# Merging B's value and output weights in seven PSUM banks instead of ten

## The chip, the core and the metric

The kernel runs on one core of a Trainium2 chip. The core has TensorE (PE in the profile; its weight loads are the row PEld), VectorE (DVE), ScalarE (ACT), GpSimd (POOL) and SyncE (SP, which here only issues DMAs). The metric is the time of one execution on the device in microseconds. Three runs of the kernel before took 254.32, 254.86 and 255.46 us; their median, 254.86 us, is the time before.

## What is computed

Two attention blocks, A and B, each on its own input of 2048 tokens and 640 features, with 32 heads of 20 features; their outputs stand side by side in the result. A is causal attention in a window of 256 keys. B is linear attention, which needs no softmax over keys:

```python
phi = lambda t: jnp.where(t > 0, t + 1, jnp.exp(t)) + 1e-6
pq, pk = phi(q), phi(k)
kv = jnp.einsum("bhsd,bhse->bhde", pk, v)
z = jnp.einsum("bhsd->bhd", pk)
num = jnp.einsum("bhqd,bhde->bhqe", pq, kv)
den = jnp.einsum("bhqd,bhd->bhq", pq, z)[..., None] + 1e-6
o = num / den
return (lambda x, *d: x.transpose(*d))(o, 0, 2, 1, 3).reshape(B, S, D) @ wo
```

## The kernel before

For B, the small matrix kv of each head (20 by 20) is known before any query is needed. So the kernel multiplies kv into the output weights once, head by head, and gets one merged weight matrix of 640 by 640. The output of B is then (phi(q) divided by its denominator) times that matrix. The function b_merge makes the merged matrix. Its 640 rows are cut into five chunks c of 128. Heads are kept in groups of six (120 rows), so a chunk overlaps two groups, and each product is two matmuls that add up in one PSUM bank: the transposed kv (kv_T) is the stationary operand, the output weights (wo) stream past it. A bank holds 512 fp32 columns. The kernel before makes the 640 columns of a chunk in two halves of 320, one bank each: ten banks, twenty matmuls, ten copies out of PSUM into w_sb["B"] (the tile wB).

All dense work of the kernel passes through the same four PSUM banks (the pool dps, tiles called dense): query, key and value projections, B's sums, the merge, the output projections, and the value products of A. Each user takes a bank with bank(), fills it on PE, and an ACT or DVE instruction copies it out and so frees it. When no bank is free, PE stands. The copy goes through evac, which keeps a running load for ACT and for DVE, in columns, and picks ACT while its load is less than DVE's plus AHEAD (600); each copy adds its columns plus COPY (160). A bank of B's query or key projection is freed later than others: phi first has ACT take the exponential (e, L286), and then DVE makes two passes (L290 on e, L293 from the bank), so it is free only after the second pass.

The order of the work is written by the kernel itself. A's scores are made in 76 tiles (S_ps, L791), which have the other four banks: PE fills them, ACT takes one exponential over all four (p, L799, the longest ACT instruction), and only then may PE write the next tile's scores. POOL masks p (L814). Two tiles later PE multiplies p with the values (L838). In the gaps between tiles PE gets dense work from a plan: the calls at(t0, t1, gen, n) spread the n banks of a generator evenly over plan times t0 to t1, one unit being about a tile; all entries are sorted by time. A credit in matmul columns is given per tile, and take() draws banks from the sorted list until it is used up, also cutting a chain of matmuls in the middle, so that a bank may begin before a score tile and end behind it. Every chain yields the columns it cost; End marks the end of a bank. The query chain of B that belongs to plan times 45 to 50 (b_q(1)), the merge, A's value projection and A's output projection alternate around the merge.

SP issues all DMAs in one queue, in the order in which the program posts them; soon() holds a DMA back until some more banks were begun. Among them are the transposes of B's phi(q) into rows by token (tok<-phi, L708), those of the finished quotients (xA<-tok, L760), those of A's normalised values (oT<-N, L879), and the reload of B's input from scratch (xB<-x_scr, L955, 640 KB). DVE multiplies tok with the reciprocal denominators (L756), and needs all five transposes of a block of 512 tokens for that.

The program as built fixes on each engine the order of all instructions, and for each chain which of the four banks it gets and so which copy it waits for.

Of the kernel before, what the change touches and what calls it, by code (L numbers as in the profile page):

```python
# [9 lines left out]
P = 128  # L10
# [7 lines left out]
DH = 20  # L18
HV = DH + 1
NG = H // 4  # L20
SB = 512
# [71 lines left out]
def kernel(  # L93
# [10 lines left out]
    nc = tc.nc  # L104
    _, S, D = A_x.shape
    KT = D // P
# [34 lines left out]
    w_sb = {}  # L141
    wo_sb = {}
# [63 lines left out]
    GH = 6  # L206
# [20 lines left out]
    def flush(before=None):  # L227

        while later and (before is None or later[0][0] <= before):
            later.pop(0)[1]()  # L230
# [9 lines left out]
    def settle(all=True):  # L240
        while posts and (all or posts[0][0] <= begun[0]):
            posts.pop(0)[1]()
# [12 lines left out]
    def evac(dst, src, n=SB, to=None):  # L255

        if to is None:
            to = "A" if load["A"] < load["D"] + AHEAD else "D"
        load[to] += n + COPY
        if to == "A":  # L260
            nc.scalar.activation(out=dst, in_=src, func=ACT.Copy)  # L261
        else:
            nc.vector.tensor_copy(out=dst, in_=src)

    def bank(wide=False):
        flush(begun[0] - 2)
        begun[0] += 1
        settle(False)
        if wide:
            return dps.tile([P, 2 * SB], BF16, name="dense")  # L270
        return dps.tile([P, SB], F32, name="dense")
# [49 lines left out]
    for c in range(KT):  # L321
        m = EXTRA * c
        while m < EXTRA * (c + 1):
            n = min(EXTRA * (c + 1) - m, DH - m % DH)
# [198 lines left out]
    GD = GH * DH  # L523
    NGR = KT + 1
    PAD = GD
    G = w_sb["B"][:, :, D : 2 * D]
    kv_T = wp.tile([P, NGR, PAD + GD + 8 * KT], BF16, name="kv_T")
# [139 lines left out]

    def b_merge():

        for c in range(KT):  # L670
            for lo in (0, D // 2):
                cols = slice(lo, lo + D // 2)
                ps = bank()
                for i in range(2):

                    at = PAD + (P - GD) * c - i * GD
                    nc.tensor.matmul(  # L677
                        ps[:, 0 : D // 2],
                        lhsT=kv_T[0:GD, c + i, at : at + P],
                        rhs=wo_sb["B"][0 : GH * DH, c + i, cols],  # L680
                        start=(i == 0),
                        stop=(i == 1),
                    )
                evac(w_sb["B"][:, c, D + lo : D + lo + D // 2], ps[:, 0 : D // 2], D // 2)
                yield End(D)

    oT_B = {}

# [57 lines left out]
    def quotients(s):  # L746


        def one(tb):
            settle()  # L750
            add_load(d=1400)
            if tb == 0:
                oT_B[s] = xp.tile([P, KT, SB], BF16, name="xA")
            v = tok_of[s][:, tb, 0:D]
            vh = v.rearrange("p (h e) -> p h e", e=DH)
            nc.vector.tensor_tensor(  # L756
                out=vh, in0=vh, in1=rden_of[s][:, tb, :, :].to_broadcast([P, H, DH]), op=ALU.mult
            )
            out = oT_B[s][:, :, tb * P : (tb + 1) * P]
            soon(lambda: nc.sync.dma_start_transpose(out=out, in_=v), 1)  # L760

        quotients_due.extend((s, tb, one) for tb in range(TPS))
# [274 lines left out]
    def at(t0, t1, gen, n):  # L1037
        for i in range(n):
            plan.append((t0 + (i + 0.5) / n * (t1 - t0), gen, i == n - 1))

    def do(t0, t1, fns):
        fns = list(fns)
        for i, fn in enumerate(fns):
            plan.append((t0 + (i + 0.5) / len(fns) * (t1 - t0), None, fn))
# [30 lines left out]
    for s, tq, td, tx in ((0, (39.5, 45), 46.3, 47.7), (1, (45, 50), 53, 54.3),  # L1075
                          (2, (52, 57), 59.4, 60.4), (3, (58, 61.6), 63.9, 64.4)):
        at(*tq, b_q(s), KT)
        at(td, td + 0.1, b_den(s), 1)
        do(tx, tx, [lambda s=s: quotients(s)])
    at(46.0, 52.8, b_merge(), 2 * KT)  # L1080
    for n, s, t0, t1 in (("A", 0, 44.5, 48.5), ("A", 1, 50.2, 54.8), ("B", 0, 54.8, 59.2),
                         ("B", 1, 60.2, 64), ("A", 2, 64.4, 68.2), ("B", 2, 69, 73),
                         ("B", 3, 73, 76)):
# [40 lines left out]
    for i, (s, parts, selects, done) in enumerate(units):  # L1124
        p = scores(s, parts, selects)
# [6 lines left out]
        if ready and ready[0][0] + LAG <= i:  # L1132
# [3 lines left out]
            _, at = ready.popleft()  # L1136
# [10 lines left out]
    while ready:  # L1147
        take(5500)
        _, at = ready.popleft()
# [36 lines left out]
```

## Time and profile before

| | |
|---|---|
| median of three runs | 254.86 us (254.32 to 255.46) |
| profiled execution | 254.11 us, of which its span is 252.4 us |
| PE busy | 241.7 us (96%), 3681 matmuls |
| ACT, DVE, POOL busy | 196.6, 167.2, 186.3 us (78%, 66%, 74%) |
| granted TensorE clock | full speed in all 40 slices |
| merge on PE (L677) | 20 matmuls, first at 162.4 us, last at 184.4 us |
| merge copies | 6 on ACT (452 ns each), 4 on DVE (474 ns each) |

A row of instructions gives line, engine, operation, names written and read, shapes, count, then busy time and the mean duration in ns of one, and the engine's idle time before it with what ended it. A row of the timeline gives start and length in us first. PE's matmuls are pipelined: a duration holds the way through the array too, so that matmuls that follow each other start closer together than they last, and a short wait can hide in the modelled end of the matmul before. Times between starts are therefore what a matmul costs PE. In the same way an ACT instruction starts somewhat before the one ahead of it ends.

Score tiles are numbered from 1 in this document: tile 51 starts at 161.20 us, tile 52 at 164.15, 53 at 166.97, 54 at 169.97, 55 at 172.78, 56 at 175.85, 57 at 178.75, 58 at 182.15, 59 at 185.05.

### The profile page before, as it was taken

How to read it: one execution, taken by the hardware profiler on the slowest of the kernel's cores; microseconds unless marked ns; L12 is line 12 of the kernel's file. 1: busy time of each engine (PE TensorE's matmuls, PEld its weight loads, DVE VectorE, ACT ScalarE, POOL GpSimd, SP SyncE). 2: the span in 40 equal slices, each digit the busy share in tenths (PEclk: the TensorE clock that was granted, in tenths of full speed). 3: DMA queues.
4: the chain of work that ended last, by engine and by line, in shares of the span. 5: the costliest groups of instructions: out<-in, count | busy, mean ns of one | idle time of the engine just before them, and what ended most of it. 6: DMA issues, size and time to landing. Idle time of an engine off the chain costs nothing.

```text
span 252.4 us, 8729 instructions
## 1 busy us (share of the span) xinstructions
PE 241.7 (96%) x3681; PEld 141.3 (56%) x3727; DVE 167.2 (66%) x311; ACT 196.6 (78%) x194; POOL 186.3 (74%) x310
## 2 busy tenths in 40 slices
PE   7999999999999999998999999999999999999994
PEld 6644456557755555466445555556455565655573
DVE  1345678777654565685664867566979688859662
ACT  3476779889867798996658877889998998999541
POOL 1226897879867898786778969888887978999800
PEclk9999999999999999999999999999999999999999
DMA  6995597799650342995459494731959389588614
GB/s 224 325 252 152 115 207 131 177 279 132 93 100 3 98 138 50 262 249 148 69 110 175 104 192 89 179 46 35 194 110 162 89 186 174 117 163 139 195 56 155
DMA packets 68412, 37.04 MB, mean 147 GB/s; under 512 B 51605, under 2 KB 67349, under 8 KB 68373
## 3 DMA queue, kind: packets, MB, share of 16 engines
q1 hardware_dynamic: 67685, 35.67, 67.2%
q10 hardware_dynamic: 688, 0.82, 0.9%
q8 instruction: 29, 0.48, 0.8%
q14 instruction: 10, 0.08, 0.1%
HBM read 14.42 MB, written 9.83 MB: 96 GB/s over the span
## 4 chain that ended last, share of the span: by engine, by line
PE 87%; issue 4%; ACT 3%; DVE 2%; DMA 2%; SPq 0%; ACTq 0%
PE dense L276 49%; PE S_ps L791 11%; PE dense L838 9%; PE dense L566 8%; PE dense L411 7%; DMA wA<-in_A_wqkv_dram 2%; ACT p L799 1%; PE first L411 1%; DVE phi L293 1%; PE dense L720 1%; DVE e L290 1%; ACT e L286 1%; PE dense L677 1%; PE dense L649 1%; PE dense L905 0%
## 5 line engine op out<-in xcount | busy, mean ns | idle before, releaser
L814 POOL TENSOR_SCALAR_AFFINE_SELECT p<-p 128x256 bf16<-128x256 bf16 (+2 forms) x280 | 176.5, 660 | 42.8 <-ACT p L799 41.3
L799 ACT ACTIVATE p<-S_ps 128x2048 bf16<-128x2048 f32 x76 | 142.8, 1879 | 34.6 <-PE S_ps L791 32.3
L276 PE MATMUL dense<-xA,wqk 128*128 128x512 bf16 x188 | 48.9, 380 | 1.4 <-issue 0.8
L791 PEld LDWEIGHTS <-kpad 20*128 20x128 bf16 (+1 forms) x1216 | 21.7, 98 | 29.6 <-issue 26.0
L791 PE MATMUL S_ps<-qpad,kpad 20*65 20x64 bf16 (+3 forms) x1216 | 33.7, 227 | 0.1
L851 DVE STREAM_TRANSPOSE T<-dense 128x512 f32<-128x512 f32 x32 | 22.8, 712 | 15.7 <-PE dense L838 15.5
L290 DVE TENSOR_SCALAR e<-e 128x512 bf16<-128x512 bf16 x40 | 18.6, 466 | 21.3 <-ACT e L286 21.1
L276 PEld LDWEIGHTS <-wqk 128*128 128x128 bf16 x200 | 17.8, 98 | 19.5 <-POOL wqk L355 0.4
L293 DVE SCALAR_TENSOR_TENSOR phi<-dense,e 128x512 bf16<-128x512 f32 x40 | 27.7, 691 | 1.6
L838 PE MATMUL dense<-p,vA 128*32 128x64 bf16 (+2 forms) x1216 | 25.9, 231 | 0.2
L276 PE MATMUL dense<-wB,xB 128*128 128x128 bf16 (+1 forms) x155 | 25.3, 297 | 0.5 <-issue 0.3
L566 PE MATMUL dense<-tok,phi 128*128 128x129 bf16 (+1 forms) x152 | 24.2, 296 | 1.5 <-issue 1.4
L276 PE MATMUL dense<-xB,wB 128*128 128x512 bf16 x91 | 24.8, 380 | 0.7 <-issue 0.5
L276 PE MATMUL dense<-wo,oT 128*128 128x128 bf16 (+4 forms) x160 | 24.3, 293 | 0.6 <-issue 0.5
L286 ACT ACTIVATE e<-dense 128x512 bf16<-128x512 f32 x40 | 23.6, 598 | 1.2 <-PE dense L276 1.0
L411 PE MATMUL dense<-wA,xA 128*128 128x320 bf16 x140 | 23.8, 300 | 0.3 <-issue 0.2
L276 PE MATMUL dense<-wB,xA 128*128 128x128 bf16 (+1 forms) x153 | 23.0, 296 | 0.6 <-issue 0.5
L838 PEld LDWEIGHTS <-vA 128*32 128x32 bf16 x1216 | 19.4, 97 | 3.8 <-issue 0.8
L261 ACT ACTIVATE osb<-dense 128x512 bf16<-128x512 f32 (+2 forms) x28 | 15.9, 581 | 5.3 <-PE dense L276 5.2
L411 PEld LDWEIGHTS <-xA 128*128 128x128 bf16 x160 | 14.9, 98 | 8.0 <-ACT xA L349 0.4
L868 DVE TENSOR_TENSOR N<-T,recA 128x320 bf16<-128x320 f32 (+1 forms) x28 | 15.5, 553 | 3.4 <-DMA wo<-in_A_wo_dram 2.5
L756 DVE TENSOR_TENSOR tok<-tok,rden 128x640 bf16<-128x640 bf16 x16 | 17.3, 1084 | 0.2 <-DMA tok<-phi 0.2
(66 smaller groups left out, 195.5 us busy)
## 6 DMA issues: line engine op xcount, KB each, us to landing
out_dram<-osb SPq DMA_DIRECT2D x7, 640.0 KB
x_scr<-xB SPq DMA_DIRECT2D x4, 640.0 KB
tok<-in_B_x_dram SPq DMA_DIRECT2D x4, 640.0 KB
xB<-x_scr SPq DMA_DIRECT2D x4, 640.0 KB
wB<-in_B_wqkv_dram SPq DMA_DIRECT2D x3, 800.0 KB
q_scr<-qpad SPq DMA_DIRECT2D x16, 60.0 KB
k_scr<-kpad SPq DMA_DIRECT2D x16, 60.0 KB
qpad<-q_scr SPq DMA_DIRECT2D x16, 60.0 KB
```

What stands on the lines that cost most here:

```text
L276: nc.tensor.matmul(dst, lhsT=lhs(kt), rhs=rhs(kt), start=(kt == 0), stop=(kt == KT - 1))
L286: nc.scalar.activation(out=view(e), in_=src, func=ACT.Exp)
L290: nc.vector.tensor_scalar(out=e[:], in0=e[:], scalar1=1e-6, scalar2=1.0 + 1e-6, op0=ALU.add, op1=ALU.min)
L293: nc.vector.scalar_tensor_tensor(out=dst, in0=src, scalar=0.0, in1=view(e), op0=ALU.max, op1=ALU.add)
L411: nc.tensor.matmul(ps[:, 0 : hh * DH], lhsT=xt[:, kt, tb * P : (tb + 1) * P], rhs=w_sb["A"][:, kt, i * hh * DH : (i + 1) * hh * DH], start ...
L566: nc.tensor.matmul(out, lhsT=pk[:, tb, c * P : (c + 1) * P], rhs=x[:, tb, lo:hi], start=(i == 0), stop=(i == len(blocks) - 1),)
L756: nc.vector.tensor_tensor(out=vh, in0=vh, in1=rden_of[s][:, tb, :, :].to_broadcast([P, H, DH]), op=ALU.mult)
L791: nc.tensor.matmul(S_ps[0:keys, j, col : col + n], lhsT=k_pad[kb // TPS][rows, g, ko : ko + keys], rhs=q_pad[s][rows, g, q0 : q0 + n], sta ...
L799: nc.scalar.activation(out=p, in_=S_ps[:], func=ACT.Exp, scale=scale)
L814: nc.gpsimd.affine_select(out=dst, in_=v, pattern=[[0, 4], [0, n], [sgn, w]], compare_op=ALU.is_ge, fill=0.0, base=base, channel_multiplie ...
L838: nc.tensor.matmul(O_ps[32 * j : 32 * (j + 1), q0 : q0 + n], lhsT=v_flat[kb // TPS % 3][:, at + j * HV : at + j * HV + 32], rhs=p[:, j, co ...
L851: nc.vector.transpose(out=T.rearrange("p b e -> p (b e)"), in_=O_ps[:])
```

## The change

The columns of a chunk are no longer halved. The first 512 columns of each chunk get a bank of their own (five banks). The last 128 columns of chunks 0 to 2 share a sixth bank, those of chunks 3 and 4 a seventh, and each of these two banks is copied out by one instruction over several chunks. A bank of the merge yields End with the columns of its two matmuls per chunk: 1024, 768 and 512 where it was 640. The seven banks are planned over 45.8 to 52.8, so one plan unit apart, where the ten were planned over 46.0 to 52.8.

```diff
+        def product(out, c, cols):
+            for i in range(2):
+                at = PAD + (P - GD) * c - i * GD
+                nc.tensor.matmul(
+                    out,
+                    lhsT=kv_T[0:GD, c + i, at : at + P],
+                    rhs=wo_sb["B"][0 : GH * DH, c + i, cols],
+                    start=(i == 0),
+                    stop=(i == 1),
+                )
         for c in range(KT):
-            for lo in (0, D // 2):
-                cols = slice(lo, lo + D // 2)
-                ps = bank()
-                for i in range(2):
...
-                evac(w_sb["B"][:, c, D + lo : D + lo + D // 2], ps[:, 0 : D // 2], D // 2)
-                yield End(D)
+            ps = bank()
+            product(ps[:], c, slice(0, SB))
+            evac(w_sb["B"][:, c, D : D + SB], ps[:])
+            yield End(2 * SB)
+        for cs in (range(0, 3), range(3, KT)):
+            ps = bank()
+            for i, c in enumerate(cs):
+                product(ps[:, i * P : (i + 1) * P], c, slice(SB, D))
+            evac(
+                w_sb["B"][:, cs[0] : cs[-1] + 1, D + SB : 2 * D],
+                ps[:, 0 : len(cs) * P].rearrange("p (c n) -> p c n", n=P),
+                len(cs) * P,
+            )
+            yield End(2 * len(cs) * P)
...
-    at(46.0, 52.8, b_merge(), 2 * KT)
+    at(45.8, 52.8, b_merge(), KT + 2)
```

More of the change, by code (lines that the diff above doesn't have):

```diff
@@ L668, in b_merge @@
     def b_merge():
-        for c in range(KT):
-            for lo in (0, D // 2):
-                cols = slice(lo, lo + D // 2)
-                ps = bank()
-                for i in range(2):
[L676 to L683, printed above, removed]
-                evac(w_sb["B"][:, c, D + lo : D + lo + D // 2], ps[:, 0 : D // 2], D // 2)
-                yield End(D)
+        def product(out, c, cols):
[8 more added lines that the diff above has]
+                )
+        for c in range(KT):
+            ps = bank()
[12 more added lines that the diff above has]
+            yield End(2 * len(cs) * P)
     oT_B = {}
```

## The prediction

> **What bounds the kernel now.** I read the page's busy times and slices first, then the chain of work that ended last, then the rows by form for the lines that change, and at the end the timeline of 160 to 200 us engine by engine.
>
> ```profile
> PE 241.7 (96%) x3681; PEld 141.3 (56%) x3727; DVE 167.2 (66%) x311; ACT 196.6 (78%) x194; POOL 186.3 (74%) x310
> PEclk9999999999999999999999999999999999999999
> PE 87%; issue 4%; ACT 3%; DVE 2%; DMA 2%; SPq 0%; ACTq 0%
> ```
>
> PE is the bound: busy 96%, the chain runs through it for 87%, at full clock in every slice. So the change is worth the columns it takes off PE, plus the stalls of PE that it removes or makes. Nothing else counts.
>
> ```profile
> L677 PE MATMUL dense<-wo,kv_T 120*128 120x320 bf16 x20 | 4.1, 300 | 0.3 <-DVE phi L293 0.3
> L261 ACT ACTIVATE osb<-dense 128x512 bf16<-128x512 f32 x24 | 14.2, 607 | 1.8 <-PE dense L276 1.7
> L261 ACT ACTIVATE wB<-dense 128x320 bf16<-128x320 f32 x6 | 2.4, 452 | 0.0
> L263 DVE CAST osb<-dense 128x512 bf16<-128x512 f32 x11 | 7.5, 683 | 3.6 <-PE dense L276 3.5
> L263 DVE CAST wB<-dense 128x320 bf16<-128x320 f32 x4 | 1.9, 474 | 0.5 <-PE dense L677 0.5
> ```
>
> The merge has one visible wait, 0.3 us for a bank that phi frees. The timeline shows it, and who is ahead of it on ACT and DVE:
>
> ```profile
> 178.86 0.61 ACT L286 ACTIVATE e<-dense 128x512 bf16<-128x512 f32 x1
> 179.35 1.89 ACT L799 ACTIVATE p<-S_ps 128x2048 bf16<-128x2048 f32 x1
> 180.50 0.69 DVE L293 SCALAR_TENSOR_TENSOR phi<-dense,e 128x512 bf16<-128x512 f32 x1
> 181.11 0.79 ACT L261 ACTIVATE wB<-dense 128x320 bf16<-128x320 f32 x2
> 181.25 0.43 PE L677 MATMUL dense<-wo,kv_T 120*128 120x320 bf16 x2 [0.34 <-DVE phi L293]
> ```
>
> PE stops until phi ends at 181.19. The exponential e of that bank ran before the long exponential p of tile 57.
>
> **The change, part by part.** *Matmuls.* Both kernels issue 20, and 6400 columns: 20 of 320, or 10 of 512 and 10 of 128. What one costs is the distance between starts. These rows (start, length, count) give it:
>
> ```profile
> 222.95 2.76 PE L276 MATMUL dense<-wo,oT 128*128 128x512 bf16 x12
> 171.73 0.84 PE L411 MATMUL dense<-wA,xA 128*128 128x320 bf16 x5
> 204.07 1.28 PE L276 MATMUL dense<-wB,xA 128*128 128x128 bf16 x20
> ```
>
> Less the length of the last one (0.38, 0.30, 0.22): 2.38/11 = 216 ns, 0.54/4 = 135 ns, 1.06/19 = 56 ns. Before: 20 x 135 = 2.70 us; after: 10 x 216 + 10 x 56 = 2.72 us. So 0.0, with bounds of -0.1 and +0.1 (5 ns on each of 20). The Trainium skill (TensorE: Matmul & The Clock Gate, Back-to-back issue gap) speaks against short matmuls: in a stream of load and matmul it gives about 81 ns at 128 columns and 131 ns at 512. By 81 ns the ten short ones would cost 0.25 us more. The rows above disagree at both sizes (56 and 216 ns, each with its own weight load), so that is left out of the sum.
>
> *Copies.* Ten of 320 (6 x 0.452 + 4 x 0.474 = 4.6 us) become three of 512 and one of 384 on ACT (3 x 0.607, and some 0.50, estimated between the two rows) and two of 512 and one of 256 on DVE (2 x 0.683, and some 0.41, on the line through 320 and 512): 4.1 us. The 0.5 us saved lies on engines that are not the bound: 0.0, as long as no bank is late. Each long copy does hold its bank 0.15 to 0.21 us longer.
>
> *The order.* The two built programs' instruction lists differ on PE only from tile 51 to tile 59; POOL's is equal. Three places matter.
>
> (a) Tile 53. At 167.46 the value product waits for ACT's wB copy (166.97 + 0.45 = 167.42): its matmuls follow tile 53's last one by 0.22 us where 0.12 is usual. In the new order that bank is freed earlier by DVE's copy of vA. Gain 0.10 (0 to 0.1).
>
> (b) Tile 57. Up to tile 56 the new order has 16 value matmuls and 6 merge ones of 512 where there were 18 and 8 of 320: 3.47 against 3.54 us. With (a), tile 57 starts at about 178.6. Then comes the difference that I rate highest: the query chain of b_q(1) is cut by tile 57, three matmuls ahead of it and two behind, where all five were ahead. Its e therefore stands behind p on ACT's queue. The new list has there p, e, wB of 512, osb, wB of 384, p. Behind tile 57 PE has the two query matmuls, a merge bank of 512, five of the output projection and the bank with six of 128: 0.36 + 0.43 + 0.43 + 1.08 + 0.34, so that it comes at 181.2 to a chain whose bank is freed by that wB copy. ACT: p starts 0.57 after its score tile (164.15 to 164.72 at tile 52): 179.2; e 1.76 after p (179.35 to 181.11): 180.95; wB 0.49 after e (178.86 to 179.35): 181.45; it ends 0.61 later: 182.05. PE resumes at 182.1 and has lost 0.85 to 0.9. Before, it lost 0.50 here (arrived at 180.75, went on at 181.25) and 0.10 on the next chain, which waited for the first of the two wB copies (181.25 to 181.62, where two matmuls take 0.27). Net +0.25. Bounds: -0.60, if ACT gets to that copy before PE asks, and +0.9, if p of tile 57 slips by one more 512-column copy ahead of it (0.61). I take +0.25: it follows from the listed order.
>
> (c) Later. The different loads make evac deal a few later copies otherwise: one of osb goes to ACT between tiles 65 and 66. There ACT had no gap: a copy at 205.39, then p at 206.10. One more copy (0.49 between starts) makes p of tile 66 0.1 to 0.2 later; it ended at 207.98 and tile 67 started at 208.16. Cost 0.05 (0 to 0.2).
>
> *SP.* One transpose tok<-phi (183.68) moves behind three oT<-N, one xA<-tok and the 640 KB reload xB<-x_scr:
>
> ```profile
> 183.68 1.21 SPq L708 DMA_TRANSPOSE tok<-phi  x1
> 184.94 3.92 SPq L879 DMA_TRANSPOSE oT<-N  x3
> 188.98 2.14 SPq L760 DMA_TRANSPOSE xA<-tok  x1
> 191.22 0.53 SPq L955 DMA_DIRECT2D xB<-x_scr  x1
> 192.19 1.21 SPq L760 DMA_TRANSPOSE xA<-tok  x1
> 192.80 0.78 DVE L756 TENSOR_TENSOR tok<-tok,rden 128x640 bf16<-128x640 bf16 x1
> ```
>
> The first product of that block (L756, 192.80) needs it. Without it in front the queue reaches xB 1.2 us earlier, at 190.0, and the transpose goes at 190.5. By the trace's landing events it landed at 186.1, 2.4 us after its issue; the transpose behind the reload landed at 196.5, 5.3 us after the reload's issue. So it now lands at 192.9 to 195.3, and DVE waits up to 2.5 us. Behind it on DVE stand recA, N, a second L756 (2.4 us from the first start to the end of all), then e and phi of the next query bank (0.39 + 0.69): phi ends at 195.3 + 3.5 = 198.8. PE asks for that bank at 198.79, plus the 0.2 of above. So the cover, DVE's idle 1.37 us before 196.62, is just enough: 0.0, and every us later than 195.4 costs PE 1 us. Bounds 0 and +1.5.
>
> *Sum*: 0.0 - 0.1 + 0.25 + 0.05 + 0.0 = +0.2 us on the profiled execution's 254.11 (span 252.4 and 1.7 around it). That execution is 0.75 us under the median of the runs shown; on the median the sum is 255.05, say 255.1. A difference of 0.5% (1.27 us) is about what a measurement can tell from none; this is a sixth of it.
>
> **The rivals.** *Fewer banks pay (faster).* If the stall of (b) vanishes, because ACT reaches e before p, 0.7 us go (0.60 and 0.10): 254.2. For it: three banks fewer ask for the four. Against it: e's place in ACT's list. It decides where the query chain ends before tile 57's p starts at 179.2. Even this is not 0.5%: PE's stalls for banks in this stretch sum to no more.
>
> *The transpose lands late (slower).* Between 165 and 190 transposes behind a 640 KB transfer took up to 5.1 us from issue to landing (177.81 to 182.94, behind out_dram). Issued at 190.5 to 192, that is 195.6 to 197.1, so PE loses 0.2 to 1.7 us: about 256.4 at the upper end. It decides from a landing after 195.4, and passes 0.5% from 196.5. Against it: nothing was added to the queues, only the order changed.
>
> *Long copies make bubbles (slower).* Five banks are held 0.15 to 0.21 us longer each; if PE stood for every one of them, 5 x 0.2 = 1.0 us, and with the sum 256.1. Against it: PE stood for a merge copy at two places only, tile 53 and behind tile 57, so it is unlikely. The Trainium skill (Perfetto Trace Analysis, Optimizing Scalar/DVE Operations) advises to break up ACT or DVE instructions that are not saturated but make bubbles on other engines, which is the opposite of this change; the wait at 181.62 for a wB copy agrees, with 0.10 us.
>
> **How the numbers follow.** Forecast, no change that can be told (254.4 to 255.7): 0.62. Faster rival 0.13, of which 0.05 over 0.5%. Late transpose 0.17, of which 0.13 over 0.5%. Long copies 0.08, nearly all over 0.5%, counted 0.07. That gives faster 0.05, same 0.75, slower 0.20. The range takes in the gain of 0.7 and 1.4 us of loss around 255.0: 254.2 to 256.4.
>
> **What the profile after would show.** 20 merge matmuls of 216 and 56 ns between starts; no wait before tile 53's value product; PE idle at about 181 to 182, ended by ACT's wB copy; e behind p at tile 57; L756 at 193 to 195.4 released by the DMA tok<-phi, and DVE's idle time before 196.6 gone; PE not idle near 199. A stall of PE there, or a landing after 196, makes the prediction wrong upward; no stall at 182 makes it wrong downward.

## The result and the profile after

The changed kernel takes 255.33 us (median of 22 executions, 254.58 to 257.49). The kernel before, measured beside it, takes 254.47 us (22 executions, 253.06 to 256.18). The ratio is 1.0037, with a 95% interval of 1.0021 to 1.0054: about 0.9 us slower. That is within the 0.5% that were set as the bound of no change, but the interval leaves out 1, so the loss is clear of the noise, and its upper end passes the bound. A second measurement on another chip gave 1.0048 (1.0036 to 1.0060), or 1.2 us.

The page of the changed kernel: busy times, the granted clock in the 40 slices, and the chain of work that ended last by engine.

```profile
PE 249.0 (97%) x3727; PEld 142.1 (56%) x3727; DVE 166.7 (65%) x310; ACT 196.7 (77%) x192; POOL 186.3 (73%) x310
PEclk9999999999999999999999999999999999999999
PE 89%; DMA 5%; DVE 3%; ACT 1%; issue 0%; SPq 0%; DVEq 0%
```

PE is still the bound, at full clock by that row. The page's busy time of PE can't be compared with the one before: 46 matmul records were missing there (3681 of 3727). The chain has DMA 5% and DVE 3%, where both had 2%: of the DMA part 3% is a weight load in the opening (wA) and 2% is tok<-phi, which the chain of before didn't hold.

The groups by form, for the merge and its copies (count, then busy time and mean ns of one):

```profile
L674 PE MATMUL dense<-wo,kv_T 120*128 120x512 bf16 x10 | 3.0, 380 | 0.0
L674 PE MATMUL dense<-wo,kv_T 120*128 120x128 bf16 x10 | 0.9, 218 | 0.0
L261 ACT ACTIVATE wB<-dense 128x512 bf16<-128x512 f32 x3 | 1.8, 599 | 0.0
L261 ACT ACTIVATE wB<-dense 128x384 bf16<-128x384 f32 x1 | 0.5, 522 | 0.0
L263 DVE CAST wB<-dense 128x512 bf16<-128x512 f32 x2 | 1.3, 664 | 0.0
L263 DVE CAST wB<-dense 128x256 bf16<-128x256 f32 x1 | 0.4, 414 | 0.0
```

No merge matmul waits any more. Where the time went is read from the starts of the score tiles, which run from the first to the last stage in both kernels. The profiled execution of the changed kernel is itself the slowest of the 22 (257.49 us): its first score tile starts 2.93 us later than before. One part of that weight load landed 2.0 us later (8.26 us against 6.29), and PE ran at half rate until 10.3 us (a matmul of 320 columns took 267 ns between starts, 136 after that), where before it did so until 4.2; the row PEclk holds no record of that stretch. That has nothing to do with the change: the instruction lists are equal there, and in a second profile of the changed kernel the same tile starts 0.8 us later than before. So every run below is set to zero at the start of tile 51, where the instruction lists begin to differ. Against the kernel before, the changed kernel then stands at -0.16 us at tile 57, +0.22 at tile 58, +0.12 from tile 59 to 63, +1.21 at tile 64 and +1.19 to the end. Two places make the loss, and the timeline shows both (columns: start, length, engine, line, instruction, and in brackets the idle time before it and what ended it):

```profile
181.33 1.88 ACT L811 ACTIVATE p<-S_ps 128x2048 bf16<-128x2048 f32 x1 [0.18 <-PE S_ps L803]
183.11 0.59 ACT L286 ACTIVATE e<-dense 128x512 bf16<-128x512 f32 x1
183.58 0.60 ACT L261 ACTIVATE wB<-dense 128x512 bf16<-128x512 f32 x1
184.24 0.38 PE L276 MATMUL dense<-wo,oT 128*128 128x512 bf16 x1 [0.66 <-ACT wB L261]
...
189.74 1.22 SPq L772 DMA_TRANSPOSE xA<-tok  x1
191.09 1.68 SPq L967 DMA_DIRECT2D xB<-x_scr  x1
192.87 1.21 SPq L720 DMA_TRANSPOSE tok<-phi  x1
194.51 1.20 SPq L772 DMA_TRANSPOSE xA<-tok  x1
198.44 0.82 DVE L768 TENSOR_TENSOR tok<-tok,rden 128x640 bf16<-128x640 bf16 x1 [3.26 <-DMA tok<-phi]
201.44 0.69 DVE L293 SCALAR_TENSOR_TENSOR phi<-dense,e 128x512 bf16<-128x512 f32 x1
202.18 0.81 PE L276 MATMUL dense<-xB,wB 128*128 128x512 bf16 x3 [0.93 <-DVE phi L293]
```

The first group is the wait that the prediction expected at tile 57: e stands behind p, the merge copy behind e, and PE behind the copy. The second is the transpose behind the reload. It is issued at 192.87, lands at 198.2 by the trace's landing events, and DVE has waited 3.26 us for it when it starts the first product of block 1 (L768, the L756 of before). Two products, e and phi later PE gets its bank, 0.93 us late. The kernel before has no wait at these matmuls:

```profile
198.79 0.81 PE L276 MATMUL dense<-xB,wB 128*128 128x512 bf16 x3
```

The queue order changed because a transpose of block 1 is held back by soon() for a number of banks, counted as they are begun. With seven banks in place of ten the same count is reached later in the plan, while the reload is posted at a fixed plan time (51.2) and so passes ahead.

### The profile page after: what moved, and what is told of

Read it like the earlier page. It is cut to its first block, busy times and chain, and to the rows that moved or that the text cites. A ratio compares the mean times of both kernels' runs of the same rounds, so it can differ in the third digit from the quotient of the medians.

```text
span 255.7 us, 8772 instructions
## 1 busy us (share of the span) xinstructions
PE 249.0 (97%) x3727; PEld 142.1 (56%) x3727; DVE 166.7 (65%) x310; ACT 196.7 (77%) x192; POOL 186.3 (73%) x310
## 4 chain that ended last, share of the span: by engine, by line
PE 89%; DMA 5%; DVE 3%; ACT 1%; issue 0%; SPq 0%; DVEq 0%
PE dense L276 50%; PE S_ps L803 10%; PE dense L566 9%; PE dense L850 8%; PE dense L411 7%; DMA wA<-in_A_wqkv_dram 3%; DMA tok<-phi 2%; DVE tok L768 1%; PE first L411 1%; PE dense L732 1%; PE dense L674 1%; PE dense L649 1%; DVE phi L293 1%; ACT e L286 0%; PE dense L917 0%
## 5 line engine op out<-in xcount | busy, mean ns | idle before, releaser
L276 PE MATMUL dense<-xA,wqk 128*128 128x512 bf16 x200 | 50.9, 380 | 0.1
L276 PE MATMUL dense<-xB,wB 128*128 128x512 bf16 x100 | 26.3, 380 | 0.9 <-DVE phi L293 0.9
L276 PE MATMUL dense<-wo,oT 128*128 128x512 bf16 (+4 forms) x165 | 25.3, 296 | 0.7 <-ACT wB L261 0.7
L276 PE MATMUL dense<-wB,xB 128*128 128x512 bf16 (+1 forms) x160 | 25.9, 300 | 0.0
L566 PE MATMUL dense<-tok,phi 128*128 128x129 bf16 (+1 forms) x160 | 25.5, 300 | 0.0
L411 PE MATMUL dense<-wA,xA 128*128 128x320 bf16 x140 | 25.0, 309 | 0.2 <-DMA wA<-in_A_wqkv_dram 0.2
L276 PE MATMUL dense<-wB,xA 128*128 128x512 bf16 (+1 forms) x160 | 24.3, 299 | 0.0
L261 ACT ACTIVATE osb<-dense 128x512 bf16<-128x512 f32 (+2 forms) x30 | 17.0, 580 | 5.4 <-PE dense L276 4.5
L411 PEld LDWEIGHTS <-xA 128*128 128x128 bf16 x160 | 15.5, 101 | 9.0 <-ACT xA L349 0.5
L768 DVE TENSOR_TENSOR tok<-tok,rden 128x640 bf16<-128x640 bf16 x16 | 16.3, 1021 | 3.4 <-DMA tok<-phi 3.3
```

What stands on the lines that cost most here:

```text
L276: nc.tensor.matmul(dst, lhsT=lhs(kt), rhs=rhs(kt), start=(kt == 0), stop=(kt == KT - 1))
L411: nc.tensor.matmul(ps[:, 0 : hh * DH], lhsT=xt[:, kt, tb * P : (tb + 1) * P], rhs=w_sb["A"][:, kt, i * hh * DH : (i + 1) * hh * DH], start ...
L566: nc.tensor.matmul(out, lhsT=pk[:, tb, c * P : (c + 1) * P], rhs=x[:, tb, lo:hi], start=(i == 0), stop=(i == len(blocks) - 1),)
L768: nc.vector.tensor_tensor(out=vh, in0=vh, in1=rden_of[s][:, tb, :, :].to_broadcast([P, H, DH]), op=ALU.mult)
```

## The experiments

Two theories stood against each other. Theory 1: the transpose that lands late makes 1.1 us of the loss (and, as a second part, ScalarE's order at tile 57 makes 0.3 to 0.4 us). Theory 2: the longer banks and copies make it.

**Seven banks, the reload one place later.**

```diff
-    for s, t0, t1 in (..., (3, 30.2, 51.2)):
+    for s, t0, t1 in (..., (3, 30.2, 51.6)):
```

> The seven banks as they are; only the 640 KB reload xB<-x_scr is planned at 51.6 instead of 51.2, which lets the transpose tok<-phi pass ahead of it on SP and moves no other instruction on any engine. Theory 1 (the late transpose is the loss): the transpose is issued near 191.1 instead of 192.87 and lands by 195.2 instead of 198.1, VectorE's wait of 3.26 us ahead of the first value product of block 1 falls under 0.5 us, PE's gap of 0.93 us at tile 64 goes, and the time falls by 0.9 to 1.1 us, to 0.9995 to 1.001 of the kernel before. Theory 2 (the longer banks and copies are the loss): PE's gaps stay where they are, the time stays at 1.0037 of the kernel before. Against both: the reload itself, one place later, becomes late for block 3's first bank; then PE waits for DMA xB there.

Measured: 254.17 us, ratio 1.0004 (0.9990 to 1.0017). The timeline of this kernel, SP and DVE:

```profile
188.77 1.91 SPq L720 DMA_TRANSPOSE tok<-phi  x1
190.78 0.53 SPq L967 DMA_DIRECT2D xB<-x_scr  x1
...
192.80 0.78 DVE L768 TENSOR_TENSOR tok<-tok,rden 128x640 bf16<-128x640 bf16 x1
```

The transpose lands at 191.9 and DVE starts the product at 192.80 without a wait, as in the kernel before. By tile starts the kernel goes through tile 64 unchanged at +0.12 and ends at +0.10. On the changed kernel's clock, which is 2.3 us later here, the transpose is issued at 191.1 and lands at 194.2, as expected. The reload lands at 195.4 in its own profile and is late for nobody. So the swap of two neighbours on SP is worth the whole 1.09 us, and being behind three oT<-N and one xA<-tok costs nothing.

**Ten banks, the transpose behind the reload.** The mirror: the kernel before, with only this DMA held back.

```diff
...
-            phi(pq[:, c, :], ps[:], then=lambda fn=to_tokens: soon(fn, 2))
+            phi(pq[:, c, :], ps[:], then=lambda fn=to_tokens, late=(s, c) == (1, KT - 1):
+                held_back.append(fn) if late else soon(fn, 2))
...
         nc.sync.dma_start(out=xB[NS + s].rearrange("p k n -> p (k n)"), in_=x_scr[s])
+        s == 3 and held_back.pop()()
```

> The kernel before, its ten banks untouched; only the fifth transpose tok<-phi of block 1 is held back until the reload xB<-x_scr has been issued, so that SP's order is the changed kernel's and every other engine's order is the one of before. Theory 1: the transpose lands near 196 instead of 186.1, VectorE waits for it 2.5 to 3.5 us, PE loses 0.9 to 1.2 us near tile 64, and the time is 1.0035 to 1.005 of the kernel before. Theory 2: no change, 0.999 to 1.001.

Measured: 255.01 us, ratio 1.0046 (1.0027 to 1.0065). The timeline of this kernel:

```profile
189.04 1.42 SPq L955 DMA_DIRECT2D xB<-x_scr  x1
190.51 1.20 SPq L708 DMA_TRANSPOSE tok<-phi  x1
...
195.82 0.83 DVE L756 TENSOR_TENSOR tok<-tok,rden 128x640 bf16<-128x640 bf16 x1 [2.94 <-DMA tok<-phi]
...
199.56 0.81 PE L276 MATMUL dense<-xB,wB 128*128 128x512 bf16 x3 [0.61 <-DVE phi L293]
```

Without any of the new banks the same wait comes, at the same place. By tile starts the loss is 0.77 us, all of it between tiles 63 and 64; the product starts at 195.82. The size is a little under what was expected by the profile, within it by the times. With both directions shown, theory 2 is out for this part.

**More bytes ahead of the late transpose.**

```diff
...
         nc.sync.dma_start(out=xB[NS + s].rearrange("p k n -> p (k n)"), in_=x_scr[s])
+        s == 3 and nc.sync.dma_start(out=more, in_=x_scr[s][:, 0 : KT * SB // 2])
```

> The changed kernel with one more copy of 320 KB, from DRAM to a DRAM buffer that nothing reads, issued on SP between the reload and the late transpose. It computes nothing else. Theory 1: the issue adds about 0.5 to 1.7 us and half a reload's transfer 2.3 to 3 us, the transpose lands 2.3 to 3.5 us later, and PE, which has no cover left, loses nearly all of it: 2 to 3.5 us more than the changed kernel, 1.012 to 1.018 of the kernel before. Theory 2: the copy is hidden, 1.0037.

Measured: 255.31 us, ratio 1.0051 (1.0032 to 1.0070): no more than the changed kernel, where 2 to 3.5 us more were expected. The timeline:

```profile
189.87 1.13 SPq L967 DMA_DIRECT2D xB<-x_scr  x1
191.05 0.58 SPq L967 DMA_DIRECT2D more<-x_scr  x1
192.06 1.23 SPq L720 DMA_TRANSPOSE tok<-phi  x1
...
196.68 1.02 DVE L768 TENSOR_TENSOR tok<-tok,rden 128x640 bf16<-128x640 bf16 x1 [2.68 <-DMA tok<-phi]
```

The copy did take its time (the reload lands at 194.65, the copy at 195.95), but the reload landed 4.8 us after its issue here and 5.9 in the changed kernel, and the transpose only 0.5 us behind the copy, where it had been 1.2 us behind the reload. So the landing isn't the sum of the bytes ahead; the theory's working of it was wrong, its place on the path was not. Of the 1.1 us by which the reload lands sooner after its issue, 0.55 is the issue itself (1.13 us in place of 1.68); what makes the rest is open.

**The transpose last.** The ten banks again, the transpose held back as in the mirror, and let go behind the fourth xA<-tok instead of behind the reload ("the run before this one" in the text below is the mirror).

```diff
...
-            soon(lambda: nc.sync.dma_start_transpose(out=out, in_=v), 1)
+            soon(lambda: (nc.sync.dma_start_transpose(out=out, in_=v),
+                 (s, tb) == (0, TPS - 1) and held_back.pop()()), 1)
```

> The kernel before with the fifth transpose tok<-phi of block 1 moved one place further back than in the run before this one: behind the reload xB<-x_scr and the fourth xA<-tok as well. No other engine's order changes. From the three runs in which this transpose was late (landing on the clock of before 195.3, 195.5 and 195.8 us; loss by the starts of the score tiles 0.71, 0.77 and 1.09 us) the loss is the landing less 194.6 to 194.7. The transpose should land at 196.0 to 196.6, and tile 64 should start 1.3 to 1.9 us later than before; time 1.005 to 1.009 of the kernel before. If the loss doesn't follow the landing (theory 2: it is something else that happens to come at tile 64), it stays at 0.7 to 1.1 us.

Measured: 256.19 us, ratio 1.0062 (1.0027 to 1.0097), so some 1.6 us, as expected. The profiled execution, at 257.93 us, lost more than its wait. Its timeline of PE, and then its busy time and granted clock in steps of 1 us (window, length, PE busy with the number of matmuls, PEclk, DMA share, GB/s):

```profile
201.09 1.40 PE L276 MATMUL dense<-xB,wB 128*128 128x512 bf16 x3 [1.91 <-DVE phi L293]
```

```profile
200.00:201.00 1.00, 0.00 (x0) 1.00 0.73 164
201.00:202.00 1.00, 0.91 (x3) 0.59 0.70 251
202.00:203.00 1.00, 1.00 (x18) 0.50 1.03 349
203.00:204.00 1.00, 1.00 (x15) 0.50 1.03 205
204.00:205.00 1.00, 1.00 (x5) 0.71 0.70 145
205.00:206.00 1.00, 1.00 (x7) 1.00 0.63 131
```

The transpose lands at 196.78, PE stands for 1.91 us, and from 201.2 to 204.6 us the granted clock is half. Tile 64 starts 2.66 us late and tile 65 3.64: 1.9 for the wait, and 1.7 for 3.4 us at half clock. Of the nine timed executions only this one shows a lowered mean clock (0.993; the others 0.998 to 1.000).

**A longer wait still**, to see whether that was an accident: one more copy of 640 KB ahead of the last transpose.

```diff
...
+                 (nc.sync.dma_start(out=more, in_=x_scr[3]), held_back.pop()())), 1)
```

> The kernel before with the fifth transpose behind the reload, behind the fourth xA<-tok and behind one more copy of 640 KB from DRAM to a DRAM buffer that nothing reads. In the run with the transpose last, PE stood for 1.91 us and its granted clock was 0.50 for some 3 us after that, so that tile 65 lost 3.64 us where the landing accounts for 1.7. Here the landing should be 2.0 to 3.5 us later still (320 KB cost 1.3 us in the run with more bytes), so that PE stands for 4 to 5.5 us. If a long wait of PE lowers the clock, the granted clock is 0.5 behind it again, for 3 us or more, and the loss by tile 66 exceeds the gap by 1.5 us or more; if the low clock of that one profile was an accident, the clock stays at 1.0 and the loss equals the gap.

Measured: 262.07 us, ratio 1.0297 (1.0277 to 1.0317). Timeline and clock of this kernel:

```profile
200.03 1.09 DVE L756 TENSOR_TENSOR tok<-tok,rden 128x640 bf16<-128x640 bf16 x1 [6.97 <-DMA tok<-phi]
...
204.61 1.44 PE L276 MATMUL dense<-xB,wB 128*128 128x512 bf16 x3 [5.48 <-DVE phi L293]
```

```profile
202.00:203.00 1.00, 0.00 (x0) 1.00 0.70 162
203.00:204.00 1.00, 0.00 (x0) 0.86 0.48 169
204.00:205.00 1.00, 0.39 (x2) 0.50 0.99 346
...
209.00:210.00 1.00, 1.00 (x3) 0.50 0.75 149
210.00:212.00 2.00, 2.00 (x19) 0.86 0.23 48
```

The transpose lands at 199.91, 3.1 us later than in the run above. PE stands for 5.48 us, the clock halves while it stands, at 203.7, and stays so until 210.6; all four executions show a mean clock of 0.987. By tile 65 the loss is 8.45 us, 3.0 more than the wait: PE works from 204.6 to 210.6 at half clock, which costs 3.0.

The landings and losses together. To be free of the opening, the landing is given against the start of tile 63 in the same run; the loss is that between the starts of tiles 63 and 64, and for the last two rows PE's wait, since the clock takes part there.

| run | landing, us after the start of tile 63 | loss, us | loss less landing |
|---|---|---|---|
| reload one place later | -4.80 | 0.00 | |
| more bytes | -1.38 | 0.71 | 2.09 |
| ten, transpose behind | -1.12 | 0.77 | 1.89 |
| changed, second profile (at the end of this section) | -1.02 | 0.87 | 1.89 |
| changed | -0.80 | 1.09 | 1.89 |
| transpose last | -0.18 | 1.91 | 2.09 |
| longer wait | +3.01 | 5.48 | 2.47 |

From 1.9 us before tile 63 each us of landing costs PE a us. On the clock of the kernel before that is 194.8 us. What the last column adds to 1.89 is the way from the landing to PE's matmul: 3.96 us in the three rows of 1.89, 4.16 with more bytes, 4.31 with the transpose last and 4.70 in the longer wait (in these two PE's wait counts 0.16 us less than the starts of the tiles do in the other rows). DVE took that much longer there: its second product of 1.06 us took 1.30 and 1.71 in the last two.

**The plan's end moved.** For the other stall.

```diff
-    at(45.8, 52.8, b_merge(), KT + 2)
+    at(45.8, 53.5, b_merge(), KT + 2)
```

> The changed kernel with the seven banks' planned end at 53.5 instead of 52.8. The transpose tok<-phi is then issued second, behind one oT<-N, as in the kernel before; and block 1's last query chain is whole before tile 57, so that ScalarE has e ahead of p again. Theory 1, with the stall at tile 57 as its second part: both stalls go, 1.1 and 0.4 us, and the time is 0.996 to 0.999 of the kernel before. If the longer copies themselves cost: 1.001 to 1.004, with PE waiting for ACT wB or DVE wB in tiles 51 to 60.

Measured: 253.84 us, ratio 0.9990 (0.9976 to 1.0004). SP's order is the one of before, e stands ahead of p, and PE's gap at tile 58 is gone: by tile starts -0.48 at tile 58, where the changed kernel stood at +0.22. At tile 60 it loses 0.18 waiting for DVE's copy of 256 columns, and ends at -0.31. The timeline of this kernel, ACT:

```profile
178.76 0.60 ACT L286 ACTIVATE e<-dense 128x512 bf16<-128x512 f32 x1
179.25 1.87 ACT L811 ACTIVATE p<-S_ps 128x2048 bf16<-128x2048 f32 x1
181.01 0.60 ACT L261 ACTIVATE wB<-dense 128x512 bf16<-128x512 f32 x1
```

**Ten banks in the same plan**, as the control of that.

```diff
-    at(46.0, 52.8, b_merge(), 2 * KT)
+    at(45.8, 53.5, b_merge(), 2 * KT)
```

> The kernel before, ten banks of 320 columns, with the same planned interval as the seven banks had in the run with the plan's end moved: 45.8 to 53.5 instead of 46.0 to 52.8. If the larger banks themselves save nothing and only the order counts, ten banks come out where seven did: 0.998 to 1.000 of the kernel before. If seven banks pay by being fewer: 1.000 or more, and the seven banks under the same plan are faster than this run by 0.2% or more.

Measured: 255.22 us, ratio 1.0021 (0.9997 to 1.0044); by tile starts nothing until tile 59, and from tile 60 on +0.83, in one wait of PE:

```profile
188.90 0.38 PE L276 MATMUL dense<-wo,oT 128*128 128x512 bf16 x1 [0.65 <-ACT osb L261]
```

By tile starts this is 1.1 us slower than seven banks in the same plan, as the theory of fewer banks had it (by the ratios, taken on two chips, the intervals just overlap). It doesn't prove that theory: the difference is one new wait behind ScalarE, where a merge bank now stands between two output banks. Under the plan of before the same ten banks have no such wait.

**Seven banks planned from 46.0 to 53.2.**

```diff
-    at(45.8, 52.8, b_merge(), KT + 2)
+    at(46.0, 53.2, b_merge(), KT + 2)
```

> The seven banks planned from 46.0 to 53.2. SP's order is the one of before, and block 1's last query chain is whole before tile 57, as with the plan's end at 53.5; the first bank comes three instructions' groups later. Theory: both stalls gone, 0.997 to 1.000 of the kernel before, with PE's largest gap between tiles 51 and 64 under 0.4 us. Against it: two wB copies stand one behind the other on ScalarE at tile 57, as in the changed kernel; if PE waits for the second, a gap of 0.5 us comes back and the time is 1.000 to 1.002.

Measured: 254.18 us, ratio 0.9995 (0.9968 to 1.0021); by tile starts -0.48 at tile 58 and -0.29 from tile 60, the same as with the end at 53.5. The two wB copies in a row on ScalarE cost nothing, once e is ahead of p.

**One copy taken from ScalarE's queue.** Seven banks, the reload at 51.6, and the fifth chunk's copy put on VectorE; the load is still counted for ScalarE, so that no later copy is dealt otherwise.

```diff
...
-            evac(w_sb["B"][:, c, D : D + SB], ps[:])
+            evac(w_sb["B"][:, c, D : D + SB], ps[:]) if c < KT - 1 else (
+                add_load(a=SB + COPY),
+                nc.vector.tensor_copy(out=w_sb["B"][:, c, D : D + SB], in_=ps[:]))
...
```

> The seven banks with the reload planned at 51.6, and in addition the fifth chunk's copy of 512 columns taken from ScalarE, where it stands behind p and e, and put on VectorE ahead of e and phi; every other instruction keeps its engine and its place. Theory (ScalarE's order at tile 57 is the stall at tile 58): PE's gap of 0.66 us there falls under 0.15 us, since VectorE is idle for 0.66 us at that place; tile 58 starts 0.4 to 0.55 us earlier, and the time is 0.997 to 0.999 of the kernel before. If the longer bank itself is what PE waits for, the gap stays at 0.5 us or more and the time at 1.000 to 1.001.

Measured: 253.96 us, ratio 0.9978 (0.9955 to 1.0000). The timeline of this kernel:

```profile
181.01 0.68 DVE L686 CAST wB<-dense 128x512 bf16<-128x512 f32 x1
...
181.74 0.38 PE L276 MATMUL dense<-wo,oT 128*128 128x512 bf16 x1
```

The same copy of the same 512 columns, 0.68 us long, frees the bank 0.5 us sooner: the wait of 0.66 us is gone from the rows (by the starts PE still loses 0.3 us there, where it lost 0.82). So most of it was the place in ScalarE's queue, and not the length of the copy. By tile starts the kernel stands at -0.31 at tile 58 and -0.41 from tile 59 on, 0.52 us ahead of the seven banks with the reload alone moved.

**This version and the changed kernel on one chip.**

> The seven banks with the reload at 51.6 and the fifth chunk's copy on VectorE, once more, beside the changed kernel on the same chip. If both stalls of the changed kernel (1.1 us by the late transpose, 0.4 us at tile 58) are what separates them, it is 0.5% to 0.7% faster than the changed kernel and 0.997 to 0.9995 of the kernel before.

> The changed kernel itself, for the comparison with the run beside it: 1.002 to 1.0055 of the kernel before, as in its first measurement; VectorE waits for tok<-phi again, and PE loses 0.7 to 1.1 us at tile 64.

Measured: 253.86 us, ratio 0.9981 (0.9963 to 0.9998), and 255.66 us, ratio 1.0048 (1.0036 to 1.0060). Dividing the two ratios, the version with both stalls removed is 0.7% faster than the changed kernel, 1.7 us; by tile starts 1.39 (-0.42 against +0.97). It has the lowest ratio and the earliest tiles of all versions, but its interval overlaps with that of the plan's end at 53.5, and it is only just clear of the kernel before: 0.2% faster, with an interval that ends at 0.9998. In its own second profile the changed kernel loses -0.16, +0.38, -0.10 and +0.87 us at the same four places.

## Why the prediction was right, and where it was wrong

It forecast 255.1 us and no change that can be told, with +0.2 us on the kernel before. The time came out so (255.33), and the change stayed under 0.5% (ratio 1.0037). But with 22 executions of each kernel it can be told from none, and it is 0.9 to 1.2 us, four to six times the sum, in the direction of the sum. That 255.1 lies so near is partly luck: it was set on a median of 254.86, and the kernel before measured 254.47 beside the changed one. Step by step:

*Matmuls, 0.0: right.* Two of 512 take 0.60 us, six of 128 take 0.50: less the last one's length 0.22 and 56 ns between starts. The 81 ns that the prediction set aside for short matmuls are not seen.

*Copies, 0.0: right.* 599 and 522 ns on ACT, 664 and 414 on DVE, where 607, some 500, 683 and some 410 were reckoned.

*(a) Tile 53, -0.10: right.* The wait for ACT's wB copy is gone. With the fewer columns ahead of it, tile 57 starts 0.16 us earlier; the prediction had it at 178.6, or 0.15 earlier.

*(b) Tile 57, +0.25: right in mechanism and size.* The order on ACT is the listed one, and PE comes back at 184.24, which is 182.1 on the clock of before, as predicted. PE lost 0.82 us by the starts of its matmuls, where 0.85 to 0.9 was predicted, and the net by tile starts from 57 to 59 is +0.28. The runs with e ahead of p take this away, and the one with the copy on VectorE takes 0.52 of the 0.82.

*(c) The later copy, +0.05: not there.* The copy did go to ACT, but cost nothing: from tile 65 to 67 the changed kernel loses nothing; it gains 0.02, and so does the kernel with ten banks and only the DMA moved (0.03).

*Sum of these: +0.2; measured +0.12 at tile 63.*

*SP, 0.0 with bounds of 0 and +1.5: the step that failed.* Its size was 0.77 to 1.09 us. The issue time was right (190.5 predicted; 190.57, 190.51 and 190.65 in three profiles, with the starts of tile 63 laid on that of the kernel before, as in the rest of this step), but by two errors that cancel: the reload ahead of it was issued at 188.8 to 189.0 and not at 190.0, and its issue took 1.4 to 1.7 us and not 0.53. Two of the terms behind it were too small. First the landing: the upper end took the 5.3 us of a transpose behind a reload from the reload's issue, and came to 195.3. It landed at 195.6 to 195.9, 5.05 to 5.35 us after its own issue and 6.6 to 7.1 after the reload's. Part of that is the reload's own longer issue. Second the cover: from the landing to the end of phi 3.5 us were reckoned, and it took 3.91 in both kernels (198.22 to 202.13, 195.60 to 199.51), since the product starts 0.2 us after the landing and e behind it takes 0.59 us from start to phi's start, where 0.39 was reckoned. The cover ended at 194.8, where the prediction had 195.4. An estimate that came out as "just enough", with a bound on one side only, should have carried some of that bound in the sum: each us past the edge is lost in full.

*The rivals.* "The transpose lands late" happened: its landing (195.6 to 197.1) and price (0.2 to 1.7 us) fit, and 0.17 was too small a chance. Against it the prediction had said that nothing was added to the queues, only the order changed; order alone was enough. "Long copies make bubbles" fell: PE waited for one long copy only, and the same copy on the other engine removed most of the wait. "Fewer banks pay" may be true of the versions without the two stalls, by 0.2% at the most that was measured (only one of their intervals, 0.9963 to 0.9998, ends under 1), and the control with ten banks leaves open how much of that is the number of banks and how much the order that each plan happens to give.

*What the profile after would show* came out for the matmuls, tile 53, the idle time at 182 and e behind p. The product did wait for the DMA; but PE was idle at tile 64, which the prediction had named as a sign of being wrong upward, and the landing was on the edge of 196, its other such sign.

## What to carry to other kernels

Where DMAs are posted after a count of some unit of work, a change of the unit's size moves them in the queue even if no DMA was touched; list the queue's order before and after, and look at each transfer that falls behind a large one. A wait that the estimate calls just covered needs a price in the sum, since past the edge it costs one for one, and behind a long one the clock may fall too. A bank held by a copy was late here by the copy's place in its engine's queue (0.52 us) more than by its length (0.15 us longer on ACT).

## What the runs showed of the hardware that was not expected

A wait of PE can cost more than itself. A wait of 0.93 us left the clock at 1.00; with one of 1.91 us the clock fell to 0.50 for 3.4 us, 2.0 us after PE had stopped, in the profiled execution, and the mean clocks of the other eight show no such fall; with one of 5.48 us it fell 4.6 us after PE had stopped, for 6.8 us, and the mean clock of all four executions is 0.987. In the clock records of these two traces every stretch at one clock, but for the last, which the end of the trace cuts off, is a multiple of 3.41 us (57, 1 and 15 times in the first; 58, 2 and 15 in the second). Cut into such steps, PE's work around the falls is this, first with the transpose last, then in the longer wait:

```profile
197.76:201.18 3.41, 1.35 (x36) 1.00 0.52 109
```

```profile
196.90:200.31 3.41, 2.07 (x64) 1.00 1.21 88
200.31:203.73 3.41, 0.00 (x0) 1.00 0.27 68
```

The clock fell behind the steps with 1.35 and 0.00 us of work and not behind the one with 2.07. So where a wait lies in its step may decide, and that would fit the one fall in nine; two falls don't show it. Nor is the wait of 1.91 us proved to be the cause: one execution each of the kernel with the copy on VectorE and of the seven banks from 46.0 to 53.2, whose profiles hold no long wait, has a mean clock of 0.993 and 0.991, and there is no trace of either. The Trainium skill (TensorE: Matmul & The Clock Gate, Why this matters for your kernels) says to keep PE from idling for more than about 3 us, since one window of idleness takes the clock back to half: the long wait agrees with it, and in the other trace the clock fell behind a shorter one.

In most profiles the sixth DMA of this row of SP, counted from the first oT<-N, was held in its issue, whichever it was: xA<-tok for 2.14 us (before) and 1.78 (plan's end moved), tok<-phi for 1.91 and 1.33 (the reload one place later, without and with the copy on VectorE), xB<-x_scr for 1.68, 1.42 and 1.13 (changed, mirror, more bytes), where these take 1.2, 1.2 and 0.53 us in the other places of the same row. The ten banks in the later plan are the exception: there the sixth took 1.21 us and the seventh, xB<-x_scr, 0.97. The reason is open. The DMAs of the row landed in the order of their issue, in the changed kernel xA<-tok at 194.03, the reload at 197.01, tok<-phi at 198.22 and the next xA<-tok at 198.81. The Trainium skill (DMA: Bandwidth & Descriptors, Queues, rings and completion order) has the completion signal of a DMA land only after all earlier writes of the same DMA engine; the order of the landings agrees with it, but no run here shows that this is why a small transpose behind 640 KB lands when it does.
